# Squares of the first halves of w1 and w2: ScalarE sums instead of TensorE diagonals, in a fused attention and MLP kernel

## The chip, the cores and the metric

The kernel runs on one core of a Trainium2 chip. A core has five engines, each with an in-order queue of its own: TensorE (PE in the profile; its weight loads are listed apart, as PEld), VectorE (DVE), ScalarE (ACT), GpSimd (POOL) and SyncE (SP, which here issues nearly all DMAs). Matrix products write to PSUM, which has eight banks here called dense0 to dense7; everything else lives in SBUF. The engines wait for one another through semaphores. The metric is the device time of one execution in microseconds; the median of several runs counts.

## The reference

One call computes, for 2048 tokens of width 512,

```
xn  = layernorm(x)
A   = infini_attention(xn, wq, wk, wv, beta) @ wo      # 32 heads of 16, 4 segments of 512 tokens
B   = gelu(layernorm(xn) @ w1 + b1) @ w2 + b2          # w1: 512 x 1792, w2: 1792 x 512
out = x + A + B
```

In the attention each segment has a masked softmax of its own; a memory matrix per head, summed over the segments before, is read with phi(q) and mixed in with sigmoid(beta).

The kernel keeps full accuracy by splitting each float32 matrix into a high and a low float16 half (h and l) and by taking three products, hh, hl and lh. Before a weight is split it is scaled by a power of two, and that power comes from the sum of the squares of the weight's elements. These sums are what the change is about. They do not appear in the reference.

## The kernel before

**Stages.** In the head of the kernel the weights are loaded, their squares summed, the power of two worked out, and the pieces scaled and split. At the same time the first tokens are normalised (`ln`, `norm_*`), turned by TensorE (`ln_out`, line 564) and split into xnT. Then the work is: projections of q, k and v (`qk_proj`, `v_nat`, line 586 through `split3`), row maxima of the logits (`m_job`, line 744 on TensorE, 751 on VectorE), softmax exponentials (`s_job`, lines 786 and 793), the product with v (`pv`, line 820), the hidden layer (`d_job`, line 586 on w1), gelu (`gelu`, line 895), its split (`h_split`), the second layer (`e_jobs`, line 935) and the output projection (line 955). Attention is cut in 16 units (4 segments by 4 groups of 8 heads); the MLP in 16 units (8 blocks of 256 tokens by two halves of the 1792 hidden columns). "1a" and "2a" are the first halves of w1 and w2 (7 of 14 pieces of 128 x 512 each), "1b" and "2b" the second halves.

**The order.** Each job has a key, such as ("D", 0, 3). `streams()` makes one list of keys per kind of job, and the string ORDER says, one letter for each job, which list gives the next job. Jobs are emitted in that order, so every engine's queue is a cut through it: an engine runs its own parts in the order of the string, and waits where an input is not there yet. BANKS gives the PSUM bank of each job in the same way. There is no scheduler at run time; where a job stands in the string is decided offline.

**Warm-up jobs.** 24 jobs ("W", function `warm`, line 500) are products of the identity with itself, two of 256 columns each. Their result is never used. They too have places in ORDER.

**Squares.** `w_square(m, k)` sums the squares of one piece. For "qk", "1b", "2b", "o" and the bias b1 it is one ScalarE ACTIVATE with the function Square and an accumulator (line 353), followed by a READ_ACCUMULATOR. For the parts in TRACES it is `w_trace`: each 128 x 128 block is taken as bfloat16 (the upper halves of its float32 words) and multiplied by itself on TensorE (line 382), all blocks into one PSUM bank; the sum of squares of each column is then on the diagonal, and one VectorE operation with the identity (line 384) takes it off. Part 1a has two such jobs of 14 blocks each, after its DMAs, and the b1 square; part 2a two jobs of 16 and 12 blocks.

**Scales and splits.** `w_scale(m)` ("wf") adds the column sums over the partitions with a product with ones (line 414, and 416 for b1), and works out the scales on VectorE in a chain of small operations (lines 388 to 438). `w_split` ("ws") then makes h and l of each piece: a "V" piece by ScalarE (line 447) and VectorE (line 448), a "G" piece by GpSimd (450), ScalarE (452) and GpSimd (454). In 1a and 2a the pieces 0, 2, 4 and 6 are "G" and 1, 3 and 5 "V".

**The queues of the head, before.** With the names of the keys (T and Tp projections of q and k, second number 1 for k; V projections of v; Xt turned tokens; D hidden layer; M row maxima; N turned phi(k); Cb rows of ratios; wm squares; wf scales; ws splits; par2 small constants), ORDER gives:

```
PE : W.0..W.15 Xt.0.0.0 W.16 wf.qk W.17 Xt.0.0.1 wm.QK.0 wm.v.0 W.18..W.20 wm.v.1 wm.QK.1 wf.v W.21 Cb.0 wm.QK.2 W.22 W.23
     Tp.1 V.0.0 wm.QK.3 wm.QK.4 par2.0 wm.QK.5 V.0.1 Xt.0.1.0 Tp.0 wf.QK Xt.0.1.1 Cb.1 wm.1a.0 wm.1a.1 T.0.1 wf.1a T.0.0
     T.1.0 wm.2a.0 wm.2a.1 D.0.0 wf.2a D.0.1 .. D.0.6 M.0.0 M.0.1 M.0.2 N.0 T.1.1 ..
ACT: wm.qk.0 wm.qk.1 Xt.0.0.0 Xt.0.0.1 ws.qk.0 ws.qk.1 ws.v.0 ws.v.1 Cb.0 ws.v.2 ws.v.3 V.0.0 V.0.1 Xt.0.1.0 Xt.0.1.1 Cb.1
     ws.QK.1 ws.QK.0 wm.1a.2 (b1) T.0.1 T.0.0 ws.1a.0 ws.1a.1 T.1.0 ws.1a.2 ws.QK.3 ws.1a.3 .. ws.1a.6 ws.2a.3 G.0 ..
SP : x(2) wv(1) qk(2) QK.0(2) v.1(2) QK.1(2) x(2) QK.2(2) beta b1 1a(4) 2a(2) ..
```

The split of a weight can begin only after its wf, and D.0.f needs the split piece f of 1a. S.0.0, the first softmax job, and everything behind it come later, from 66 us on.

Of the kernel before, what the change touches and what calls it, by code (L numbers as in the profile page):

```python
# [9 lines left out]
F32 = mybir.dt.float32  # L10
# [49 lines left out]
def streams():  # L60
# [78 lines left out]
    "hxahhhlhk6hkkhwxbhhlchkhdhhe6hhhfh6auhfi8$hks7hhl$8$h7%%j%8%hbhgRtc88dmr8ieRfg8fmjn&v9&9!&y&#9(nCzA)((CD++*)X9"  # L139
    "+2*BB((D)o,!-*X(,(X3)*,X,9.XoXXYZ#0F1FFPy-,FZz.0Fp1F,R49F/oZF4-.!0R,1-.Z4F//F4XABXB#0Q/F4$4/=p14=4PUE44FF::4;="  # L140
    "=4G<4GFGX=FG2XG3FHF22:4;HI>:IHq?aIIFGb@:GXc>XGH>FGyFFGXXz?d:<fFeYXC;HHAEZXIQIDI0I><GGG>J1HXX:>KX4GBBLGZfP0MHCF"
    "FHqQNOIII1;IDGF44GGFiZ<0[34X>1GaZFFyHF@?zGF4H4@X0?FBFHIY@I1I3bI4c[4A4[FEJBK4XZ40X1X4ZX0[1L44GGGXXGFeF4Z4d0HffP"
    "1a4FZGF4H4]H014FYMFF44N]Z4yFzQOIIjII]0GF4CAF]G4XD4TFEXbGG1G4^B4PHHHZB0XIIII_GJ1GKGXHVyFZLG0Gz4i41C4AHFFIHTMNI^"
    "IZOIDG01G44XHXGF44GFGHXBFFYFIHIIIBFFRR4_FFFF44X44EGZJF0KLc1GX4MNOHR4iSZeGGGRdFHH0FIII1QIFZFGSGFFUPHyAGUG5HzGSX"
    "FWS2EI0H1BIIQ53IGGJVZKLC2DGTGGXX4MHPN0WX444VBHfHOfIIIQIFGF44GG14XFG3GY4HjH4HZ04FFF4yF1F5IaIIIZFz0F4CX41bX42DXX"
    "F4BEJZ4401X4Z0cTXXKe14ABU5344i4XYdGZGLF4XMGFF4H440UGF2G414ZHNPXFFIHIOIIQ0GGFX3XGG1HFXWFFZGH0f44fVF1ZHX4Y4y04E1"
    "IzIZIIJGG44KCA4LG0aGG4BHDjTMNH44H4W44OI1IIBIGGGXVXbPGHFGZyFFzHFHIIIcI0R1AJRZF01KZFFLRCFFFX0BRDeXFdfEfBX4X44GM1"
    "GGH4aU4NT4XFGGOS4FHFYFQHIIIIWXFZ5GFSP04G1G4X4FZbGGS4H2HFFH0FIQIIiI1yzZS0FJKVEAcCT4D4LXGMG4PX1BHGUGGNZX3X444HWV"
    "0HIIBIOIGF5G41444GFGXFGjF2yFHzHFHFIYQZeIII0JCK4U41ZUTX4DBX40FF3dF1Z4X041XLX4FZ0f45M1X4EWVA44Bf4N45GGG4X4FFGYHX"
    "4O4ZFGHF44H2440XPFFI1IIIFFGZy20F1ZGHF44XX04z13GG3ZHG4FHCXXTX0414UIEjIDQYIIBJGGK444GGHLGMBHX4Z4XXXINIHIOIFGF401"  # L150
# [8 lines left out]
    "01234567012345670123456713072134627341257034275036125470361254370125403725340725364072316420731460271024637102"  # L159
    "46530274163045127301245701367205136472013642713642076143201746317204617240672406532146532710465372104573201457"  # L160
    "32014562014205634205136420571360257143026714302514307251403751264037521640375231640723164073164072536140725361"
    "40275430612754130675421630542631054261054327654132764153276415032761450376145076145076152074153674316507431650"
    "71436257143263527014305127643207516320753620741625074136250741253607451320745130267451360245136042513674251367"
    "45213670452103647210364720364507326450732640532647032614750326174032641073256417023546170354617305617305614307"
    "61423076513427364517351062473510625417365241760524176024576102437610243716024375413602154376021576403157640135"
    "74061357406135671403275164032751643027543402751340257136402731640273674301274360136274103764214032765403276510"
    "327650413615304651302451243705124037254137254012375640213574021734502617350261735406"
# [17 lines left out]
def infini_mixer_kernel(ctx: ExitStack, tc: tile.TileContext, x, wq, wk, wv, wo, beta, w1, b1, w2, b2, out):  # L185
# [65 lines left out]
    AM = {"v": 8, "1a": 10, "1b": 12, "2a": 17, "2b": 19, "o": 23}  # L251
    am = cst.tile([P, 28], F32, name="am")
# [74 lines left out]
    def w_square(m, k):  # L327
        if m in TRACES and (m, k) != ("1a", 2):
            return w_trace(m, k)
# [3 lines left out]
        else:  # L333
            to = am[:, AM[m] + k:AM[m] + k + 1]
            a = m[0]
            if m == "1a" and k == 2:
                r, to = b1t, am[:, 16:17]
            elif m[1:] == "a":
                r = flat(a)[:, 1024 + 1792 * k:2816 + 1792 * k]
            elif m[1:] == "b":  # L340
                o = 1024 + 512 * FH
                r = flat(a)[:, o + 1536 * k:o + (1536, 2560)[k]] if k < 2 else stage[a][k - 2]
            elif k == 0:
                r = flat(a)[:, 1024:2048]
            else:
                r = stage[a][2 if m == "v" else k - 1]
# [6 lines left out]
        A.activation(junk.bitcast(BF)[:, :r.shape[1]], r, AF.Square, accum_out=to)  # L353
# [3 lines left out]
    def w_trace(m, k):  # L357
# [50 lines left out]
    def w_scale(m):  # L408
# [6 lines left out]
        if m == "1a":  # L415
            T.matmul(p[:, 1:2], ones, am[:, 16:17], start=True, stop=True)
# [642 lines left out]
```

## Time and profile before

| | |
|---|---|
| median of 3 runs | 690.71 us (690.51 to 691.18) |
| the profiled execution's own time | 689.64 us |
| span of the profile | 687.9 us |
| TensorE busy | 680.4 us (99%), 5883 products |
| VectorE / ScalarE / GpSimd busy | 502.6 / 472.7 / 348.9 us |
| granted TensorE clock | 0.998 over the span |
| HBM read / written | 37.77 / 17.05 MB |

The span is the time from the first to the last instruction in the trace; the device time holds some 1.7 us more. A product on TensorE is shown with the time from its start until its result is out, and the next one begins before that; so a group's time in a list (twelve products of 256 columns: 1.47 us) holds one such tail, and the cost of one more product in a row is read from two groups of different counts. A busy TensorE is thus not a TensorE without gaps; whether it waits is read from the list of waits and from the chain that ended last. For an instruction with an idle time before it, the list gives that time in brackets with what ended it.

### The profile page before, as it was taken

How to read it: one execution, taken by the hardware profiler on the slowest of the kernel's cores; microseconds unless marked ns; L12 is line 12 of the kernel's file. 1: busy time of each engine (PE TensorE's matmuls, PEld its weight loads, DVE VectorE, ACT ScalarE, POOL GpSimd, SP SyncE). 2: the span in 40 equal slices, each digit the busy share in tenths (PEclk: the TensorE clock that was granted, in tenths of full speed). 3: DMA queues.
4: the chain of work that ended last, by engine and by line, in shares of the span. 5: the costliest groups of instructions: out<-in, count | busy, mean ns of one | idle time of the engine just before them, and what ended most of it. 6: DMA issues, size and time to landing. Idle time of an engine off the chain costs nothing.

```text
span 687.9 us, 15912 instructions
## 1 busy us (share of the span) xinstructions
PE 680.4 (99%) x5883; PEld 393.8 (57%) x5883; DVE 502.6 (73%) x1615; ACT 472.7 (69%) x877; POOL 348.9 (51%) x574
## 2 busy tenths in 40 slices
PE   8999999999999999999999999999999999999997
PEld 6765664666554666665545555665654446475543
DVE  5899968897896668786595786977477765787522
ACT  4588998787856666678826747666956545857960
POOL 5595769664536354563652426435363325247562
PEclk9999999999999999999999999999999999999999
DMA  9788243222120441512222023330502122240001
GB/s 276 225 209 238 82 113 93 64 63 73 57 39 16 109 117 36 121 17 80 55 61 81 16 72 78 85 88 20 114 24 63 56 65 77 62 102 17 4 16 61
DMA packets 52890, 55.85 MB, mean 81 GB/s; under 512 B 4990, under 2 KB 41868, under 8 KB 52812
## 3 DMA queue, kind: packets, MB, share of 16 engines
q1 hardware_dynamic: 50508, 50.64, 26.9%
q0 software_dynamic: 2304, 4.20, 3.8%
q8 instruction: 46, 0.75, 0.5%
q14 instruction: 32, 0.26, 0.1%
HBM read 37.77 MB, written 17.05 MB: 80 GB/s over the span
## 4 chain that ended last, share of the span: by engine, by line
PE 96%; DVE 1%; DMA 1%; POOL 0%; ACT 0%; issue 0%; SPq 0%; POOLq 0%; DVEq 0%
PE dense L586 40%; PE dense L935 21%; PE dense L820 11%; PE dense L744 6%; PE dense L786 6%; PE dense L955 6%; PE dense L684 2%; PE dense L564 1%; DMA wqs<-in_A_wq_dram 1%; PE dense L700 1%; PE dense L651 1%; PE dense L382 1%; PE dense L721 1%; PE dense L757 0%; DVE xnT L568 0%
## 5 line engine op out<-in xcount | busy, mean ns | idle before, releaser
L751 DVE CUSTOM_DVE_ANT_0 dense<-dense,mask 128x384 f32<-128x384 f32 (+3 forms) x512 | 233.8, 528 | 28.5 <-PE dense L744 24.3
L793 ACT ACTIVATE pt<-dense,qkcs 128x512 f32<-128x512 f32 (+1 forms) x384 | 204.3, 628 | 45.1 <-PE dense L786 44.7
L935 PE MATMUL dense<-w2s,hT 128*128 128x512 f16 x672 | 166.7, 380 | 0.0
L586 PE MATMUL dense<-xnT,w1s 128*128 128x256 f16 x1344 | 160.0, 273 | 0.0
L807 POOL TENSOR_SCALAR_AFFINE_SELECT pt<-pt 128x256 f32<-128x256 f32 x256 | 100.3, 424 | 109.3 <-ACT pt L793 108.8
L586 PEld LDWEIGHTS <-w1s 128*128 128x128 f16 x1344 | 129.3, 98 | 29.4 <-issue 5.9
L909 POOL TENSOR_TENSOR hT<-hh,hT 128x512 f16<-128x512 f32 x64 | 67.2, 1050 | 101.4 <-ACT hT L907 89.6
L935 PEld LDWEIGHTS <-hT 128*128 128x128 f16 x672 | 60.8, 98 | 68.0 <-issue 14.0
L820 PE MATMUL dense<-pt,vt 128*32 128x512 f32 (+3 forms) x1024 | 77.2, 436 | 0.0
L751 DVE DVE_READ_ACCUMULATOR2_ANT mc<- 128x1 f32 x512 | 73.9, 144 | 0.0
L888 DVE SCALAR_TENSOR_TENSOR hT<-dense,sc,cb 128x512 f32<-128x512 f32 x64 | 43.6, 681 | 33.8 <-PE dense L586 33.5
L820 PEld LDWEIGHTS dense<-pt,vt 128*32 128x32 f32 x1024 | 31.4, 109 | 40.9 <-issue 32.4
L786 PE MATMUL dense<-qst,kst 50*128 50x384 f16 (+3 forms) x512 | 52.0, 298 | 0.0
L744 PE MATMUL dense<-kst,qst 48*128 48x384 f16 (+3 forms) x512 | 51.9, 298 | 0.0
L905 POOL TENSOR_SCALAR hh<-hT,sc 128x512 f32<-128x512 f32 x64 | 42.3, 661 | 17.5 <-ACT hT L895 11.4
L851 POOL TENSOR_TENSOR nN<-nN,oT 128x512 f32<-128x512 f32 x16 | 20.3, 1272 | 52.6 <-DVE oT L663 52.6
L907 ACT ACTIVATE hT<-hh 128x512 f16<-128x512 f32 x64 | 37.5, 585 | 13.7 <-POOL hh L905 13.7
L895 ACT ACTIVATE hT<-hT,b1t 128x256 f32<-128x256 f32 x112 | 46.5, 498 | 0.2
L955 PE MATMUL dense<-wos,oT 128*128 128x512 f16 (+2 forms) x204 | 44.0, 367 | 0.9 <-DVE acc L957 0.7
L586 PE MATMUL dense<-xnT,wks 128*128 128x512 f16 (+1 forms) x252 | 44.4, 329 | 0.0
L586 PE MATMUL dense<-xnT,wqs 128*128 128x512 f16 (+1 forms) x252 | 44.2, 328 | 0.0
L586 PE MATMUL dense<-wvs,xnT 128*128 128x512 f16 x192 | 43.6, 379 | 0.0
(229 smaller groups left out, 836.9 us busy)
## 6 DMA issues: line engine op xcount, KB each, us to landing
kst<-kd SPq DMA_DIRECT2D x32, 192.0 KB
qst<-qd SPq DMA_DIRECT2D x32, 192.0 KB
qd<-hl SPq DMA_DIRECT2D x36, 128.0 KB
kd<-hl SPq DMA_DIRECT2D x33, 128.0 KB
acc<-in_A_x_dram SPq DMA_DIRECT2D x16, 256.0 KB
acc<-in_B_b_dram POOLq DMA_DIRECT2D x16, 256.0 KB, 4.5
out_dram<-acc SPq DMA_DIRECT2D x15, 256.0 KB
xt<-in_A_x_dram SPq DMA_DIRECT2D x14, 256.0 KB
```

The source lines that it names most:

```text
L586: T.matmul(p, ws(k, a), xs(k, b), start=i == 0, stop=i == 3 * KT - 1)
L744: T.matmul(p[:, o:o + n], stk[i, 0][r, t, P * qb:P * qb + P], stk[i, 1][r, t, :n], start=True, stop=True)
L751: V.tensor_tensor_reduce(p[:, o:o + n], p[:, o:o + n], mask[:, 512 - n:], 1.0, -3e38, OP.add, OP.max, mc[i][:, 4 * b + t, qb:qb + 1])
L786: T.matmul(p[:, o:o + n], stk[i, 1][r, t, P * kb:P * kb + P], stk[i, 0][r, t, P * kb:], start=True, stop=True)
L793: A.activation(pt[i, 4 * b + t][:, OFF[kb]:OFF[kb] + n], p[:, c:c + n], AF.Exp, scale=qkcs[:, 1, i % NG:i % NG + 1])
L807: G.affine_select(v, v, pattern=[[0, 2], [1, P]], compare_op=OP.is_ge, fill=0.0, base=0, channel_multiplier=-1)
L820: T.matmul(p[32 * c:32 * c + 32, P * kb:], vt[s, kb][:, 4 * g + c, 16 * odd:16 * odd + 32], pt[i, 2 * c + odd][:, OFF[kb]:OFF[kb] + LEN[kb ...
L888: V.scalar_tensor_tensor(hz[:, f0:f + 1, :], p[:, :256 * n].rearrange("p (f c) -> p f c", f=n), col(CG + fh), cbt[hf].unsqueeze(1).to_broa ...
L895: A.activation(hz[:, f, :], hz[:, f, :], AF.Gelu_apprx_tanh, bias=b1t[:, fo:fo + 1])
L909: G.tensor_tensor(hT[:, z, 1, :], hht[j, c], hT[:, z, 0, :], op=OP.subtract)
L935: T.matmul(p, t[:, u, P * a:P * a + P], w2s[:, fo, v, :], start=fi == 0 and n == 0, stop=fi == FH - 1 and n == 2)
L955: T.matmul(p[:, c], o[:, u, P * b:P * b + P], wos[:, g, v, c], start=i == 0, stop=i == 3 * NG - 1)
```

## The change

TRACES keeps only QK and v. The squares of 1a are now four ScalarE sums, one for each of the four DMAs of 1a (128 rows of w1 each; on the chip seven runs of 128 elements per partition, 896 in all), and the b1 square is the fifth job of the part. Those of 2a are two ScalarE sums, one for each DMA (2048 and 1536 elements per partition). `am`, the tile of partial sums, has three more columns. In `w_scale` the product with ones now takes four columns for 1a and two for 2a where it took one, and a VectorE reduction adds these (`n > 1`). The 56 products of blocks and the two operations that took the diagonal off go.

ORDER and BANKS are new for the first 391 jobs (393 in the new string); the remaining 1330 jobs stand in the same order. The number of warm-up jobs is the same.

```
-TRACES = ("QK", "v", "1a", "2a")
+TRACES = ("QK", "v")
-SQUARES = {"qk": 2, "QK": 6, "v": 2, "1a": 3, "2a": 2, "1b": 4, "2b": 4, "o": 3}
+SQUARES = {"qk": 2, "QK": 6, "v": 2, "1a": 5, "2a": 2, "1b": 4, "2b": 4, "o": 3}
-    AM = {"v": 8, "1a": 10, "1b": 12, "2a": 17, "2b": 19, "o": 23}
-    am = cst.tile([P, 28], F32, name="am")
+    AM = {"v": 8, "1a": 26, "1b": 12, "2a": 17, "2b": 19, "o": 23}
+    am = cst.tile([P, 31], F32, name="am")
...
-        if m in TRACES and (m, k) != ("1a", 2):
+        if m in TRACES:
             return w_trace(m, k)
...
-            if m == "1a" and k == 2:
-                r, to = b1t, am[:, 16:17]
-            elif m[1:] == "a":
-                r = flat(a)[:, 1024 + 1792 * k:2816 + 1792 * k]
+            if m == "1a":
+                r, to = (flat(a)[:, 1024:1024 + 512 * FH].rearrange("p (f r c) -> p f r c", f=FH, r=KT)[:, :, k], to) if k < 4 \
+                    else (b1t, am[:, 16:17])
+            elif m == "2a":
+                r = flat(a)[:, 1024 + 2048 * k:(3072, 1024 + 512 * FH)[k]]
...
-        A.activation(junk.bitcast(BF)[:, :r.shape[1]], r, AF.Square, accum_out=to)
+        junk = junk.bitcast(BF)[:, :r.shape[1] * (P if len(r.shape) == 3 else 1)]
+        if len(r.shape) == 3:
+            junk = junk.rearrange("p (f c) -> p f c", c=P)
+        A.activation(junk, r, AF.Square, accum_out=to)
...
-        n = 4 if h else 3 if m == "o" else 1
+        n = 4 if h or m == "1a" else 3 if m == "o" else 2 if m == "2a" else 1
...
-            T.matmul(p[:, 1:2], ones, am[:, 16:17], start=True, stop=True)
+            T.matmul(p[:, 4:5], ones, am[:, 16:17], start=True, stop=True)
```

The new ORDER gives these queues in the head:

```
PE : W.0..W.9 Xt.0.0.0 W.10 W.11 Xt.0.0.1 wm.QK.0 W.12 wf.qk W.13 wm.v.0 wm.QK.1 wm.v.1 wf.v wm.QK.2
     Tp.1 wm.QK.3 wm.QK.4 Cb.0 V.0.0 wm.QK.5 V.0.1 wf.QK Xt.0.1.0 Xt.0.1.1 par2.0 W.14..W.16 Tp.0 T.0.1 T.0.0 W.17 W.18
     wf.1a W.19..W.23 T.1.0 Cb.1 N.0 D.0.0 D.0.1 wf.2a D.0.2 .. D.0.5 M.0.0 D.0.6 M.0.1 M.0.2 M.0.3 T.1.1 ..
ACT: wm.qk.0 Xt.0.0.0 wm.qk.1 Xt.0.0.1 ws.qk.0 ws.qk.1 ws.v.0 .. ws.v.3 Cb.0 V.0.0 wm.1a.0 wm.1a.1 V.0.1 Xt.0.1.0 Xt.0.1.1
     ws.QK.1 wm.1a.2 ws.QK.0 wm.1a.3 T.0.1 wm.1a.4 (b1) T.0.0 wm.2a.0 ws.1a.0 ws.1a.1 wm.2a.1 ws.1a.2 ws.1a.3 ws.QK.2 T.1.0
     Cb.1 ws.1a.4 N.0 ws.1a.5 ws.QK.3 ws.2a.1 ws.2a.0 ws.1a.6 G.0 ..
DVE: .. Xt.0.0.0 Xt.0.0.1 wf.qk par2.1 wm.v.1 ws.qk.0 wf.v ws.qk.1 ws.v.0 ws.v.1 wm.QK.4 ws.v.2 ws.v.3 ..
SP : x(2) wv(1) qk(2) QK.0(2) v.1(2) QK.1(2) QK.2(2) x(2) 1a(2) beta b1 1a(2) 2a(2) ..
```

On GpSimd the first norm root (X.0.0.2) now comes ahead of the memset of the ones in vt (const.2); before it came behind it.

66 lines of the change are left out of this document (28 added, 38 removed).

## The prediction

> **What bounds the kernel now.** I read the page first, then the list of who waited for whom on TensorE, then the chain that ended last for the first 45 us, which is where the order changes. From the page, the chain by engine, and the complete list of TensorE's waits:
>
> ```profile
> span 687.9 us, 15912 instructions
> PE 96%; DVE 1%; DMA 1%; POOL 0%; ACT 0%; issue 0%; SPq 0%; POOLq 0%; DVEq 0%
> ...
> PE dense L500 <- POOL ident masks.py:199: 1.4, 1, 1.4
> PE dense L564 <- DVE xt L535: 1.0, 1, 1.0
> PE dense L955 <- DVE acc L957: 0.7, 1, 0.7
> PE dense L414 <- DVE dense L384: 0.3, 1, 0.3
> ```
>
> Columns of the waits: total us, times, longest. TensorE waits four times, 3.4 us in all; three of the four lie in the first 13 us. Behind them it works without a wait up to the last stage. So what counts is the sum of TensorE's work, warm-ups included. The chain of the first 45 us (start, length, what; count of instructions):
>
> ```profile
> 2.70 5.93 DMA wqs<-in_A_wq_dram
> ...
> 11.88 0.66 DVE wks L448
> ...
> 13.48 0.22 PE dense L527 x2
> ...
> 24.38 1.60 PE dense L382 x28
> ...
> 31.56 1.60 PE dense L382 x28
> 33.16 1.31 PE dense L586 x12
> 34.47 0.12 PE dense L414 x2
> 34.59 7.88 PE dense L586 x72
> 42.47 0.76 PE dense L744 x8
> 43.23 0.58 PE dense L651 x4
> ```
>
> Until about 9 us the path is the load of q's weights; from 14 us it is TensorE, and the two blocks of 28 products that the change removes (L382 on w1s and w2s) stand on it with 1.60 us each. The order of time of TensorE shows what warm-ups fill and what they cost (start, length, what, count):
>
> ```profile
> 1.43 6.18 PE L500 MATMUL dense<-ident 128*128 128x256 bf16 x32 [1.43 <-POOL ident masks.py:199]
> 8.62 0.63 PE L564 MATMUL dense<-ident,xt 128*128 128x128 f32 x4 [1.01 <-DVE xt L535]
> 9.09 0.38 PE L500 MATMUL dense<-ident 128*128 128x256 bf16 x2
> ...
> 11.03 0.82 PE L500 MATMUL dense<-ident 128*128 128x256 bf16 x6
> ...
> 14.20 1.47 PE L586 MATMUL dense<-xnT,wks 128*128 128x256 f16 x12
> ```
>
> Two products take 0.38 us and six 0.82, so one more costs (0.82 - 0.38) / 4 = 0.11 us and one warm-up job 0.22 us. Tp.1, the first projection, starts at 14.20 us behind all 24 warm-up jobs.
>
> Finally the other engines by stretch, and ScalarE's queue around the change:
>
> ```profile
> 10.00:20.00 10.00, 9.68 (x91) 7.20 (x90) 9.00 (x30) 5.35 (x9) 2.16 (x7) 1.00 1.16 310
> 20.00:30.00 10.00, 10.00 (x95) 8.07 (x94) 7.97 (x33) 5.45 (x12) 5.85 (x10) 1.00 0.75 246
> 30.00:40.00 10.00, 10.00 (x101) 8.48 (x99) 8.80 (x19) 7.17 (x13) 8.54 (x8) 1.00 0.75 179
> 40.00:50.00 10.00, 9.98 (x71) 5.58 (x70) 9.04 (x34) 9.53 (x18) 9.09 (x11) 1.00 0.83 217
> 50.00:60.00 10.00, 10.00 (x98) 5.58 (x97) 9.96 (x40) 8.49 (x18) 7.78 (x9) 1.00 0.96 262
> ...
> 18.30 0.60 ACT L711 ACTIVATE vt<-dense 128x512 f32<-128x512 f32 x1 [1.70 <-PE dense L586]
> 21.84 0.60 ACT L711 ACTIVATE vt<-dense 128x512 f32<-128x512 f32 x1 [2.94 <-PE dense L586]
> ...
> 24.20 0.60 ACT L567 ACTIVATE xnT<-dense 128x512 f16<-128x512 f32 x1 [1.27 <-PE dense L564]
> ...
> 35.09 0.63 ACT L452 ACTIVATE w1s<-w1s 128x512 f16<-128x512 f32 x1 [1.15 <-POOL w1s L450]
> ...
> 40.22 1.28 ACT L895 ACT_TABLE_LOAD   x1
> ...
> 51.08 1.47 ACT L353 ACTIVATE w1s<-w1s 128x1536 bf16<-128x1536 f32 x1
> 52.45 0.19 ACT L353 ACTIVATION_READ_ACCUMULATOR w1s<-w1s 128x1 f32 x1
> ...
> 55.65 1.04 ACT L353 ACTIVATE w1s<-w1s 128x1024 bf16<-128x1024 f32 x1
> ```
>
> Columns of the stretches: length, then busy us of PE, PEld, DVE, ACT, POOL, granted clock, DMA share, GB/s. ScalarE is idle for 4.65, 4.55 and 2.83 us in the three stretches from 10 to 40 us, 12.0 us together; from 40 us it is nearly as full as VectorE and TensorE. Three limits lie close together there.
>
> **The change, part by part.**
>
> *Products removed:* 2 x 1.60 = 3.20 us of TensorE, all of it on the chain. The two reductions of `w_scale` stay off it: the sums over four and two columns are added on VectorE, 0.2 us each at most (a small operation, below), against two removed diagonal operations; the product with ones takes four columns for one at the same count. I take 0 for both. Their cover is VectorE's idle 1.2 us of 30 to 40; without it they would cost 0.4.
>
> ```profile
> 26.20 0.29 DVE L384 SCALAR_TENSOR_TENSOR dense<-dense,ident 128x128 f32<-128x128 f32 x1
> 26.41 0.14 DVE L384 DVE_READ_ACCUMULATOR dense<-dense,ident 128x1 f32 x1
> ...
> 19.21 0.16 DVE L973 TENSOR_REDUCE eo<-half 128x2 f32<-128x8 f32 x1
> ```
>
> *Warm-ups moved:* the count is the same, but W.14 to W.23 now stand behind Tp.1: 10 x 0.22 = +2.2 us on a TensorE that does not wait there. This is the term that takes most of the gain back. It costs nothing only where TensorE would have waited anyhow; it is worth all of 2.2 where it would not.
>
> *Tp.1 earlier:* fewer jobs stand ahead of it. What it waits for is the low half of k's first piece on VectorE, done at 11.88 + 0.66 = 12.54 us before. In the new order VectorE has the small constants and v's diagonal ahead of that operation (about 0.6 and 0.35 us), so about 13.5 us, and Tp.1 at 13.6: -0.6 us. On GpSimd the norm root no longer sits behind the memset of vt (1.07 us), so the first turned tokens come about 1.3 us sooner, but the sum of q's squares waits for its load in any case. Bounds: -1.1 (13.1, when v's diagonal hides) and +0.5 (below).
>
> ```profile
> 3.68 1.07 POOL L229 MEMSET vt<- 128x256 f32 x4
> ...
> 6.85 0.24 POOL L483 TENSOR_SCALAR nw<-ag 128x2 f32<-128x2 f32 x1
> ```
>
> *Cb.0 behind Tp.1:* two turned rows, 0.22 us (L527 above): +0.2. N.0 and M.0.0 come ahead of D.6 and would have to be done anyway: 0.
>
> *Loads:* SP's queue has q's and k's last pieces ahead of the second pair of x, and beta and b1 between the DMAs of 1a. The bytes ahead of w2's last piece are the same and the queue streams without a gap; the page of 12 to 30 us in 40 slices of 0.45:
>
> ```profile
> GB/s 330 347 346 340 339 300 296 293 309 287 288 299 298 264 295 300 281 273 280 310 238 211 287 289 339 355 373 396 355 387 405 373 287 159 146 46 0 0 50 132
> ```
>
> It ends near 28 us. One DMA of 1a (448 KB, at about 290 GB/s) takes some 1.6 us; the products read the last one at 24.2, so the four are there by about 19.4, 21.0, 22.6 and 24.2 at the latest, and 2a by 28. The turned second tokens need x two pieces later (512 KB, some 1.7 us); VectorE reaches that x at 17.3 us before and not sooner now, so I take 0, and +0.3 for the one place where I see TensorE wait: between V.0.1 and the turned second tokens, whose norm follows v's splits on VectorE. Bounds 0 and 1.
>
> *ScalarE's new work:* from the rows with 1536 and 1024 elements one element costs (1.47 - 1.04) / 512 = 0.84 ns, and from 51.08 to the instruction behind the read at 52.55 is 1.47 us, so the read is nearly hidden. A sum of 896 costs 0.95 us, of 2048 1.9, of 1536 1.47: 4 x 0.95 + 1.9 + 1.47 = 7.2 us, into 12.0 us of idle time. The pieces of w1 land one after another, and the first two sums lie in the wait of 2.94 us ahead of the second V. Behind them queue, in order, the turned tokens, the splits of q and k, T.0.1 and T.0.0; the two sums of 2a stand right among the splits of 1a. I put ScalarE's queue together from 23.3 us (the split ws.QK.1, behind the second turned tokens) to the split ws.1a.6: eleven splits at 0.52 to 0.6 (6.3 us), four sums and b1's (5.6), T.0.1, T.0.0, T.1.0, Cb.1 and N.0 (2.9), and the rest of the starts, 15.7 us in all, so 39.0 us if it waits for nothing. GpSimd needs some 1.2 us more for the low half of piece 6: 40.2. TensorE wants it at D.0.6. That job began at 34.59 + 7.88 - 1.31 = 41.16 before; the sum below, with N.0 (0.58) and half of the M products (0.4) now ahead of it, puts it at about 41.0. So ScalarE's cover is 0.8 us: hidden, with little left.
>
> *Sum:* -3.2 + 2.2 - 0.6 + 0.2 + 0.3 = -1.1 us. The profiled execution took 689.64 us, 1.07 below the median of the runs shown, so it would be 688.5 there, and **689.6 us** against the median of 690.71. The rest, from 43 us on, has the same work; I see no wait in the old order there, so the new one can win nothing by order alone, except from VectorE's side, a rival below.
>
> *The clock, by the rows and by a rule.* The first 32 warm-up products take 6.18 us: (6.18 - 0.38) / 30 = 0.19 us for each, where later ones take 0.11. So TensorE starts slow. Now only 20 such products run, from 1.43 to about 5.3 us, and then TensorE pauses until about 7.3 (8.62 less the 1.3); if it is slow still, the jobs up to Tp.1 (8 turned blocks, 4 warm-ups, 28 products of blocks: some 4 us at the fast rate) take up to 3 us more, of which about 1 would be on the way to Tp.1; from these rows I carry 0, with +1.05 as the upper end. The Trainium skill ("TensorE: Matmul & The Clock Gate", Part 1) says that the array runs at half rate until it has been busy through one free-running window of about 3.4 us. By that rule the shorter burst may miss its window, and the fast rate may come only between 10 and 14 us: an estimate from that page would be a sum of -0.1 instead of -1.1. The row agrees that the start is slow; no row shows what a pause does to it.
>
> **The rivals.**
>
> *A, the forecast:* TensorE stays the bound, -1.1, from -1.8 to -0.4.
>
> *B, VectorE was the real limit from 43 us on, and it comes forward.* For it: 9.96 of 10 us busy from 50 to 60. The first row maximum now needs D.0.5 and not D.0.6 and N.0: TensorE reaches M.0.0 1.31 us sooner on top of 1.1, minus 0.58 for N.0, and the last product of D.0.6 is then VectorE's to do later (0.5). Against it: TensorE shows no wait there, and cannot lose work by it. It gives about -1.9, 688.8 us.
>
> *C, the saving is given back in the head:* the slow clock, or ten warm-ups plus a wait. It gives about -0.1, 690.6 us: the order does what it says, nothing is won.
>
> *D, ScalarE's queue becomes the bound.* Its place is the stretch from T.0.1 to D.0.6; its price is one for one what ScalarE waits there beyond 0.8 us. For it: before, it was idle for 2.83 us of 30 to 40 alone, and 1.27 us in one wait ahead of that, each time for an engine that is no faster now, and the sums of 2a delay the splits behind them by 3.4 us. Against it: with more work queued, a wait turns into work. At 3.3 us of waits it gives 3.3 - 0.8 - 1.1 = +1.4 and decides for slower; at 3.7, less than those two together, +1.8, 692.5 us.
>
> **How the numbers follow.** A change of 0.2%, 1.4 us, is about what measuring this kernel can tell from none. A has 0.36, and a third of it (0.11) lies beyond -1.4; B 0.20; C 0.24; D 0.20. Faster: 0.11 + 0.20 = 0.31. Same: 0.25 + 0.24 = 0.49. Slower: D, 0.20. The likeliest case by itself reaches from 688.9 to 690.3. For the range I take the lower bounds of Tp.1 and of the wait, and B's gain, together about -2.9 (687.8), and above D's 692.5: 687.8 to 692.5 leaves out the far ends of B and D, some 2 in 10.
>
> **What would show it.** The two groups of 28 products are gone, and TensorE is busy 3 us less or so. Tp.1 starts near 13.6 and not at 14.2; D.0.6 begins near 41. There is no idle time of TensorE between Tp.1 and D.0.6 beyond the 0.3. ScalarE has four sums of 896 near 0.95 us, is busy some 7 us more before 40 us, and loads the gelu table near 39 to 40. Rival C would show in the clock: warm-up and turned products at 0.19 us and more up to 11 us and beyond. D would show idle time of TensorE ahead of D jobs, released by GpSimd's or ScalarE's split of w1s. The prediction is wrong if TensorE waits by more than 1 us anywhere between 15 and 130 us, where before it never does, or if the ten warm-ups lie in time that would have been idle.

## The result, and the profile after

The changed kernel took 695.92 us (median of 6 runs, 695.55 to 700.42) against 690.63 for the kernel before on the same chip: ratio 1.007, 95% interval 1.0043 to 1.0097. Run again with more rounds it took 696.5 against 691.24 (ratio 1.0083, 1.0056 to 1.011). It is slower by some 5 us; 689.6 was forecast, with 692.5 as the upper end.

The first profiled execution of the changed kernel was its slowest (700.42). So the reading below goes by the profile of `e1_changed_again` (696.02 us), where not said otherwise. Most code lines of the changed kernel are six below those of before (586 is 580 there, 744 is 738; ScalarE's squares are 357 for 353); those of e10 and e11 are four above. Its page, with the span and the chain by engine:

```profile
span 694.3 us, 15813 instructions
...
PE 87%; DVE 5%; DMA 3%; ACT 1%; SPq 1%; issue 1%; POOL 1%; POOLq 0%; DVEq 0%; ACTq 0%
```

Its list of who waited for whom on TensorE (total us, times, longest), without what lies in the first 14 us and two entries of 0.3 and 0.2 us at its end:

```profile
PE dense L715 <- ACT vt L705: 1.6, 1, 1.6
...
PE dense L580 <- DVE phk L632: 1.2, 1, 1.2
...
PE dense L645 <- DVE phk L632: 0.7, 1, 0.7
PE dense L949 <- DVE acc L951: 0.7, 1, 0.7
PE dense L738 <- DVE mc L745: 0.7, 1, 0.7
PE dense L780 <- DMA qst<-md: 0.6, 1, 0.6
```

The chain was 96% TensorE before; now 87%, with more of VectorE (5% for 1%) and DMA (3% for 1%) in it. Before, TensorE had one wait behind 13 us, the 0.7 at the end. Now there are two above 1 us, and they are of other kinds: V.0.3 (L580) waits for VectorE, K.0 (L715) for ScalarE. Busy times in stretches of 10 us (length, then PE, PEld, DVE, ACT, POOL, granted clock, DMA share, GB/s):

```profile
10.00:20.00 10.00, 8.97 (x80) 6.20 (x81) 9.00 (x32) 6.39 (x12) 1.48 (x5) 1.00 1.12 303
20.00:30.00 10.00, 10.00 (x83) 8.09 (x82) 6.99 (x31) 9.71 (x21) 6.09 (x10) 1.00 0.89 288
30.00:40.00 10.00, 9.26 (x78) 7.47 (x77) 7.87 (x16) 9.62 (x17) 7.06 (x8) 1.00 0.66 181
40.00:50.00 10.00, 9.78 (x70) 5.34 (x69) 10.00 (x30) 8.19 (x15) 8.19 (x9) 1.00 0.60 162
50.00:60.00 10.00, 7.20 (x79) 3.88 (x74) 9.97 (x29) 6.29 (x12) 6.04 (x8) 1.00 0.97 251
```

TensorE is idle for 2.8 us of 50 to 60, where before it had 10.00; VectorE is full from 40 on. ScalarE has the forecast work in 20 to 40 and is *less* busy behind it than before: it waits there too.

Where the time goes is read from TensorE's start on named jobs. The table has the time of before and, for each profiled execution, how much later (+) or earlier (-) it starts. At D.0.6 the new order has N.0 and M.0.0 (about 1 us) already done; from M.1.0 on the jobs done are the same, and from about 128 us the order of TensorE is.

| us | Tp.1 | D.0.6 | M.1.0 | at 128 | last product |
|---|---|---|---|---|---|
| before | 14.20 | 41.00 | 64.10 | 128.1 | 684.02 |
| changed (e1) | -0.34 | +0.70 | +3.09 | +5.11 | +6.66 |
| e6, warm-ups first | -0.81 | -0.44 | +0.77 | +1.94 | +2.91 |
| e12, and early load | -0.23 | +0.15 | -0.34 | +0.79 | +2.24 |
| e15, and old order from M.1.0 | +0.06 | -0.14 | -0.78 | -0.58 | +1.08 |
| e17, changed, old order from M.1.0 | -1.02 | +0.01 | +2.38 | +3.22 | +3.32 |
| e10, old order, no squares | +0.35 | -1.17 | +1.28 | +1.72 | +2.16 |
| e11, and early load | +1.22 | -0.30 | +0.07 | +0.10 | +0.36 |
| e13, before with early load | +0.47 | +0.47 | +0.46 | +0.45 | +0.53 |

Each row is one execution. Those of e10 (691.81) and e17 (693.0) are the shortest of their kernels, 2.1 and 2.2 us below the median, so what their other executions lost beyond the row is not seen.

So the head of e1 came out near the forecast: D.0.6 at 41.70 for about 41, which is 0.3 us won, jobs done ahead included, where 1.1 was forecast. The loss has three places: 43 to 64 us, 64 to 128 us, and about 1.5 us behind that.

### The profile page after: what moved, and what is told of

It is laid out like the page before. It is cut to its first block, busy times and chain, and to the rows that moved or that the text cites. A ratio compares the mean times of both kernels' runs of the same rounds, so it can differ in the third digit from the quotient of the medians.

```text
span 698.7 us, 15813 instructions
## 1 busy us (share of the span) xinstructions
PE 682.5 (98%) x5827; PEld 392.4 (56%) x5827; DVE 508.0 (73%) x1613; ACT 478.8 (69%) x889; POOL 347.1 (50%) x574
## 4 chain that ended last, share of the span: by engine, by line
PE 88%; DVE 4%; ACT 2%; DMA 2%; POOL 2%; issue 1%; POOLq 0%; SPq 0%; ACTq 0%; DVEq 0%
PE dense L580 35%; PE dense L929 19%; PE dense L814 10%; PE dense L949 6%; PE dense L780 6%; PE dense L738 5%; PE dense L678 2%; PE dense L558 1%; DVE dense L745 1%; PE dense L694 1%; PE dense L645 1%; DMA xt<-in_A_x_dram 1%; DVE w2s L442 1%; POOL kst L239 1%; PE dense L715 0%
## 5 line engine op out<-in xcount | busy, mean ns | idle before, releaser
L745 DVE CUSTOM_DVE_ANT_0 dense<-dense,mask 128x384 f32<-128x384 f32 (+3 forms) x512 | 233.8, 527 | 31.7 <-PE dense L738 25.5
L580 PE MATMUL dense<-xnT,w1s 128*128 128x256 f16 x1344 | 160.4, 273 | 0.0
L580 PEld LDWEIGHTS <-w1s 128*128 128x128 f16 x1344 | 129.3, 98 | 29.9 <-issue 6.1
L929 PEld LDWEIGHTS <-hT 128*128 128x128 f16 x672 | 61.2, 98 | 68.8 <-issue 15.5
L580 PE MATMUL dense<-wvs,xnT 128*128 128x512 f16 x192 | 43.7, 379 | 1.2 <-DVE phk L632 1.2
L580 PE MATMUL dense<-xnT,wks 128*128 128x512 f16 (+1 forms) x252 | 44.4, 329 | 0.2 <-DVE mc L745 0.2
L580 PE MATMUL dense<-xnT,wqs 128*128 128x512 f16 (+1 forms) x252 | 44.4, 329 | 0.0
```

The source lines that it names most:

```text
L580: T.matmul(p, ws(k, a), xs(k, b), start=i == 0, stop=i == 3 * KT - 1)
L745: V.tensor_tensor_reduce(p[:, o:o + n], p[:, o:o + n], mask[:, 512 - n:], 1.0, -3e38, OP.add, OP.max, mc[i][:, 4 * b + t, qb:qb + 1])
L929: T.matmul(p, t[:, u, P * a:P * a + P], w2s[:, fo, v, :], start=fi == 0 and n == 0, stop=fi == FH - 1 and n == 2)
```

## The experiments

**The changed kernel again, and its two parts alone.** `e1_changed_again` is unchanged.

> The changed kernel as it is, for a second profile, since the profiled execution took 700.42 us and the median of its runs was 695.92. Theory P (port): three VectorE instructions with two SBUF operands or in a fast form (L626 at 49.2, the low half of w2's piece 3 at 52.7, C2 of wf.2b at 74.8 us) are held while GpSimd works back to back, and TensorE waits behind each; it expects 695.5 to 696.5 us and at least two of these three stretched again, to over twice their usual length. Theory Q (load): ScalarE's 7.2 us of new squares make it the bound behind the head; it expects ScalarE without idle time between 45 and 75 us and TensorE's waits released by ScalarE.

Measured: 696.5 (695.26 to 701.72), as above. Two of the three operations that theory P names are stretched again (1.40 and 2.52 us, below); the third took 1.10. ScalarE has idle time, 3.47 us in one wait (below), where theory Q expected none.

`e2_new_order_products` keeps the new ORDER, and the products on TensorE:

```
-TRACES = ("QK", "v")
+TRACES = ("QK", "v", "1a", "2a")
+    # all 28 blocks at the last of a part's squares jobs; the b1 square stays on ScalarE
```

> The new order, but the squares of 1a and 2a as products on TensorE again (all 28 blocks where the last square stood) with the two diagonal operations; ScalarE has its old load. Q expects the waits behind 43 us to vanish: 690.6 + 3.2 - 1.1 = 692.7 us. P expects that the VectorE instructions of the order stay beside GpSimd's runs and that the waits stay: 698 to 700 us, 3 more than the changed kernel.

`e3_old_order_squares` is the other half: the old ORDER, the squares on ScalarE at the landings.

```
 old ORDER, new TRACES and SQUARES
-.. Cb.1 wm.1a.0 wm.1a.1 (b1) T.0.1 wf.1a T.0.0 T.1.0 wm.2a.0 wm.2a.1 D.0.0 wf.2a D.0.1
+.. wm.1a.0 wm.1a.1 V.0.1 .. wm.1a.2 Tp.0 .. wm.1a.3 (b1) T.0.1 T.0.0 wf.1a wm.2a.0 T.1.0 wm.2a.1 D.0.0 D.0.1 wf.2a
```

> The old order and its banks with all warm-ups ahead of Tp.1, and the squares of 1a and 2a on ScalarE: the jobs of the squares, wf.1a and wf.2a are moved to where the pieces have landed, T.0.0 and D.0.1 ahead of them, nothing else. Q expects 7.2 us more on ScalarE to cost as in the changed kernel: 692 us or more. P expects the old neighbourhood of VectorE and GpSimd behind 43 us to stay clear: 690.6 - 3.2 + some 1.7 of waits at D.0.0 and D.0.2 = 689.1, between 687.5 and 690.5.

Measured: 694.37 (ratio 1.0055, 1.0034 to 1.0076) and 696.44 (1.0075, 1.0052 to 1.0097). Each half alone is slower than before, and the new order is 2.1 us *faster* with the products on TensorE than with the squares on ScalarE. e2 lies between what the two theories expected, and 1.7 us above the 692.7 that the forecast's own terms give, with no wait of TensorE above 0.7 us behind 14 us. e3 lies 7 us above theory P's 689.1. For the squares in the old order, TensorE's waits say why:

```profile
PE dense L580 <- POOL w1s L448: 2.7, 2, 2.2
PE dense L408 <- ACT w1s L357: 1.7, 1, 1.7
...
PE dense L408 <- ACT w2s L357: 0.8, 1, 0.8
```

The first and the third lie in the head: the splits of w1 come too late for D jobs, and wf.2a waits for the square of w2. The second lies at 66 us, in wf.1b, and returns below.

**The squares left out.** Is TensorE's work in the head worth anything? Two kernels do no squares of the first halves at all. Their partial sums are constants, so the scales do not come from the data:

```
+    G.memset(am[:, 10:11], 0.173)   # e10; the like for 1a and 2a in e9
...
+        if m == "2a" or m == "1a" and k < 2:
+            return
```

> The new order with the squares of 1a and 2a left out altogether: the columns of partial sums are filled with a constant of about their size by three small memsets at the start, so ScalarE has 7.2 us less to do and TensorE no products. Q expects the waits behind 43 us gone and 690 us or less. P, as far as it holds the order itself at fault, expects 694 to 696; a P in which the squares only shift VectorE's operations beside GpSimd's runs expects other waits than in the changed kernel, in sum smaller, 691 to 694.

> The old order with the products of 1a and 2a left out and the partial sums filled with constants, nothing in their place: the most that this change could win. If TensorE's work is what counts in the head, as my sum has it, 690.6 - 3.2 = 687.4 us. If another engine's chain (wf.1a and the splits on ScalarE, VectorE and GpSimd) stands right behind TensorE there, less: 688.5 to 690.6, with waits of TensorE at D jobs.

Measured: 693.26 in the new order (1.0031, 1.0013 to 1.005) and 693.92 in the old one (1.0039, 1.0017 to 1.0061). So in the new order the squares on ScalarE cost some 3 us against none at all (e1 against e9, 696.5 and 693.26), as much as was to be saved on TensorE. It shows behind the head: from D.0.6 to M.1.0, with the same jobs in the same order, the profile of e9 takes 23.1 us, that of e2 23.5 and that of e1 25.5.

e10 came out above all that was expected of it. It is the run that overturns the forecast's premise: 3.2 us of TensorE's work are taken out of the old order, nothing is put in, and the kernel gets 3.0 us *slower*. The table shows how: from Tp.1 to D.0.6 it is 1.5 us faster; by M.1.0 it is late. ScalarE, TensorE and SP's queue of that run (start, length; waits: total, times, longest):

```profile
60.21 0.63 ACT L357 ACTIVATE w1s<-rc 128x512 bf16<-128x512 f32 x1 [4.18 <-DMA rc<-in_B_w_dram]
```

```profile
62.01 0.38 PE L418 MATMUL dense<-am,ones 128*128 128x4 f32 x2 [1.79 <-ACT w1s L357]
```

```profile
SPq L312 <- DMA kd<-rc: 3.4, 1, 3.4
```

The same in the kernel before:

```profile
57.14 0.63 ACT L353 ACTIVATE w1s<-rc 128x512 bf16<-128x512 f32 x1 [0.35 <-DMA rc<-in_B_w_dram]
```

```profile
SPq L310 <- DMA kd<-rc: 1.7, 1, 1.7
```

TensorE waits in wf.1b, the scale of w1's second half, for the square of a piece that is loaded into the tile rc. That tile also carries a projection on its way to DRAM. So SP's queue may issue the load only when the store kd<-rc is done, and ahead of the load stand 1.28 MB of w2. Before, the last of these squares was done at 59.3 and wf.1b began at 60.8:

```profile
60.84 0.28 PE L414 MATMUL dense<-am,ones 128*128 128x4 f32 x2
```

In e10 SP waited longer for the store, and the piece came 3 us later: 0.9 us of it because the load was issued later (53.03 for 52.15), the rest between issue and landing. And TensorE came sooner. In both kernels the DMA engines are full meanwhile; the stretches 54 to 60 of e10 (columns as above):

```profile
54.00:56.00 2.00, 2.00 (x18) 1.00 (x17) 2.00 (x9) 2.00 (x4) 2.00 (x3) 1.00 1.03 334
56.00:58.00 2.00, 2.00 (x21) 1.79 (x19) 2.00 (x13) 0.03 (x1) 2.00 (x3) 1.00 1.04 237
58.00:60.00 2.00, 2.00 (x42) 0.98 (x40) 1.97 (x8) 0.00 (x0) 0.14 (x1) 1.00 1.04 205
```

A DMA share of 1.03 to 1.04, and ScalarE with nothing to do.

**The waits of the changed kernel.** Its longest ones follow VectorE operations that took far longer than their like. VectorE and GpSimd of `e1_changed_again`:

```profile
49.29 1.40 DVE L626 TENSOR_SCALAR phk<-phk,qksc 128x512 f32<-128x512 f32 x1
...
52.82 2.52 DVE L442 SCALAR_TENSOR_TENSOR w2s<-w2s,sc 128x512 f16<-128x512 f32 x1
```

```profile
49.24 1.16 POOL L903 TENSOR_TENSOR hT<-hh,hT 128x512 f16<-128x512 f32 x1 [1.71 <-ACT hT L901]
...
52.01 1.66 POOL L444 TENSOR_SCALAR w2s<-w2s,sc 128x512 f32<-128x512 f32 x2
53.35 1.43 POOL L448 TENSOR_TENSOR w2s<-w2s 128x512 f16<-128x512 f32 x1
```

and TensorE behind them:

```profile
51.47 2.75 PE L580 MATMUL dense<-wvs,xnT 128*128 128x512 f16 x12 [1.21 <-DVE phk L632]
...
58.10 0.27 PE L715 MATMUL dense<-vt,pkn 128*32 128x32 f32 x8 [1.59 <-ACT vt L705]
```

The first VectorE operation begins 0.05 us behind a GpSimd instruction and ends 0.3 us behind its end; the second begins beside two and ends 0.56 us behind the end of the third. V.0.3 waits for the first by way of VectorE's next operation (L632). K.0 waits for the second by way of ScalarE, which stands still for it and then has a split and a square of w1's second half to do ahead of the copy that K.0 needs:

```profile
55.37 0.72 ACT L441 ACTIVATE w2s<-w2s,sc 128x512 f16<-128x512 f32 x1 [3.47 <-DVE w2s L442]
```

The same jobs in the same order, some 2 us sooner, in `e6_warmups_first` (below):

```profile
47.58 0.48 DVE L626 TENSOR_SCALAR phk<-phk,qksc 128x512 f32<-128x512 f32 x1
...
50.19 0.98 DVE L442 SCALAR_TENSOR_TENSOR w2s<-w2s,sc 128x512 f16<-128x512 f32 x1
```

There V.0.3 and K.0 do not wait. The pair of 1.40 and 2.5 us between 48 and 59 us is in all profiles of kernels that have the squares on ScalarE and warm-ups behind Tp.1 (e1, e4, e14, e17 and the first profile; e5 has the 1.40 alone) and in none of e2, e6, e9, e12, e15 and e16. The Trainium skill ("SBUF — State Buffer", Who interferes with whom) has VectorE and GpSimd share a port pair, which VectorE takes in its two-port modes and of which it uses the reading side for a second SBUF input; whoever issues first holds it for a whole instruction. These rows agree, and show more: the hold here spans several GpSimd instructions in a row. That a shared port is what holds these operations is read from the overlap in time; no run parted it from other causes. And a held operation by itself need not cost: before has one of 1.58 us for a usual 0.7 (L448, at 26.41 us), and no wait of TensorE behind it.

Two runs took such waits away. In the first profile one such operation, a scale of 128 x 1, took 2.84 us where its like take 0.2 (and 1.10 us in e1, the same kernel):

```profile
74.80 2.84 DVE L432 SCALAR_TENSOR_TENSOR sc<-sc 128x1 f32<-128x1 f32 x1
```

`e4_c2_one_operand` gives it one SBUF tensor operand:

```
-            V.scalar_tensor_tensor(col(C2 + h), col(f), float(2 ** -26), col(B1F + h), op0=OP.mult, op1=OP.mult)
+            V.tensor_scalar(col(C2 + h), col(f), float(2 ** -26), col(B1F + h), op0=OP.mult, op1=OP.mult)
```

> The changed kernel, and only C2 (one column, f * 2^-26 * b1f) computed with the second factor as a scalar operand instead of as a second tensor from SBUF; same result, same order. P expects this instruction at 0.2 to 0.3 us in place of up to 2.84, TensorE's wait of 2.4 us at 76 to 79 us gone, and 693.5 to 694.5 us. Q expects no change: 695.9.

`e5_three_apart` is e4, and in addition V.0.3 and K.0 exchange their banks, and two splits of w2 on VectorE and GpSimd move behind the load of w1's last pieces:

```
-.. M.0.4 ws.2a.3 H.0.2.0 A.0.1 H.0.2.1 wl.1b.2 M.0.5 ws.2a.4 M.0.6 Tr.1.1 ws.2a.5 ..
+.. M.0.4 H.0.2.0 A.0.1 H.0.2.1 wl.1b.2 M.0.5 M.0.6 Tr.1.1 ws.2a.3 ws.2a.4 ws.2a.5 ..
-K.0 and V.0.3: banks 4 and 6
+K.0 and V.0.3: banks 6 and 4
```

> The changed kernel with the three places of TensorE's waits behind 43 us taken apart and nothing else: V.0.3 and K.0 exchange their PSUM banks (V.0.3 no longer waits for the k tile of Tw.1.1), the split of w2's piece 3 stands three jobs later, next to that of piece 5, and C2 has a scalar operand. Theory P (VectorE instructions held beside GpSimd's runs, TensorE waits behind them): the low half of piece 3 back from 2.5 to under 1.2 us, the waits of 1.2, 1.6 and 0.7 us gone, 696.0 - 3.5 = 692.5 us in executions in which the clock stays fast. Theory Q (ScalarE's load): the waits come back at neighbouring jobs, 695 to 696.5.

Measured: 696.27 (1.0067, 1.0043 to 1.0091) and 696.38 (1.0076, 1.0051 to 1.0101): nothing won. In the profile of e4 the operation took 0.21 us, and the 2.51 stayed; in that of e5 the 2.5 was gone as well, but other waits had come in its place, at the neighbours:

```profile
PE dense L580 <- DVE mc L745: 3.0, 2, 2.8
PE dense L715 <- ACT vt L705: 1.1, 1, 1.1
PE dense L738 <- ACT pt L787: 0.9, 1, 0.9
```

So taking these waits away by themselves won nothing, and in e5 they moved. That they moved because VectorE is full there fits the busy times, but no run gave VectorE less to do.

**The warm-ups.** `e6_warmups_first` puts all 24 ahead of Tp.1 and changes nothing else:

```
-.. W.9 Xt.0.0.0 W.10 W.11 .. W.13 .. Tp.1 .. W.14 W.15 W.16 Tp.0 .. W.17 W.18 wf.1a W.19 .. W.23 T.1.0 ..
+.. W.9 .. W.15 Xt.0.0.0 W.16 W.17 .. W.18 wf.qk W.19 .. W.20 W.21 .. W.22 W.23 wf.v .. Tp.1 ..
```

> The changed kernel with all 24 warm-up jobs ahead of Tp.1 again: 16 ahead of the first turned tokens, the others in TensorE's waits between there and wf.v; nothing else moves. My sum priced the ten warm-ups behind Tp.1 at 2.2 us on a TensorE that does not wait: 693.8 us. If they stood in waits anyway: no change in the undisturbed executions, 695.5 to 696.5. Either way, if the slow clock of the head makes the executions at 698 us and above, these go, and the granted clock shows no half-rate stretch before 20 us.

Measured: 692.87 (1.0031, 1.0017 to 1.0045), 3.6 us less than the changed kernel. The table splits the 3.8 us between the two profiles: 0.5 by Tp.1, 0.7 on to D.0.6, 1.2 on to M.1.0 (the two waits above are gone; a wait of 1.59 us in wf.1b has come), and 1.4 from there to the end. The granted clock is 1.00 in the heads of both, and their turned blocks take 0.60 us, so none of this is the clock. In other executions of the changed kernel it is. That kernel has 20 warm-up products at its start and then waits for the first tokens; before and in e6 there are 32. The first profile of the changed kernel, TensorE and the stretch behind it (last columns: granted clock, DMA share, GB/s):

```profile
7.66 0.79 PE L558 MATMUL dense<-ident,xt 128*128 128x128 f32 x4 [2.36 <-DVE xt L529]
```

```profile
8.00:12.00 4.00, 4.00 (x30) 0.58 1.14 322
```

and the same stretch of e1:

```profile
8.00:12.00 4.00, 2.91 (x37) 1.00 1.15 324
```

Behind a wait of 2.36 us the clock is 0.58. In e14 it was 2.22 us and 0.54, in e4 1.97 and 0.60, while in e1, with 1.80 us, it stayed at 1.00, and so it did in e17 (1.95) and in before (1.01). In e9, with 1.90 us, four turned blocks took 1.06 us for a usual 0.60 as late as 9.5 us, though the clock reads 1.00 there. So the length of the wait alone does not decide it. This is rival C's mechanism: it struck in four of the eight profiles with 20 products at the start (the others: e1, e2, e5, e17), and Tp.1 came at 15.0 to 15.5 us in three of these four. The forecast carried 0 for it.

**The load of w1's last pieces.** Four kernels take away what this load waits for: it goes to two tiles that are free then, and right behind the other loads of w1's second half.

```
-                stage["1"] = [sb.tile([P, 512], F32, name=t)
-                               for t in ("rc", "ame")]
+                stage["1"] = [sb.tile([P, 2, 512], F16, name="oT", bufs=4).rearrange("p a c -> p (a c)").bitcast(F32)
+                              for j in range(2)]
-.. wl.1b.1 .. wl.2b.0 .. wl.1b.2 ..
+.. wl.1b.1 wl.1b.2 .. wl.2b.0 ..
```

(The expectation of e11 speaks of wf.1a where wf.1b is meant.)

> The order of before without products or squares of the first halves (their partial sums are constants, so the output is not the reference's, as in the run e10_old_order_no_squares), and in addition the loads of the last two pieces of w1 go into two tiles of the tag oT instead of the tags rc and ame, and are issued right behind the other loads of w1's second half. In e10_old_order_no_squares these two loads waited 3.4 us on SP's queue for the store kd<-rc out of the same tile, stood behind 1.28 MB of w2, and ScalarE idled 4.18 us and TensorE 1.8 us (at wf.1a's second part, L418) for them. Theory L (what TensorE saves in the head is lost at w1's second half, because its last two pieces land too late): the square of rc starts ahead of 57 us (60.2 before this edit), the wait of 1.8 us is gone, M.1.0 starts at 63.3 (65.4 less 2.1), time 691.8, that is within 0.3% of before and 2.1 below 693.92. Theory N (every engine is about as full, a wait that is removed turns up at a neighbour): M.1.0 at 64.5 or later, time 693.2 or more.

> e6_warmups_first (692.87: the changed kernel with all 24 warm-ups ahead of Tp.1) with the same move of the loads of w1's last two pieces. There TensorE waited 1.6 us at L408 for the squares of these pieces and ScalarE 1.4 and 0.75 us for their landing. Theory L: the wait is gone, 691.3 (692.87 less 1.6). Theory N: 692.3 to 693.4.

> The kernel before with the same move of the loads and nothing else. Its TensorE has no wait between 42 and 68 us, so theory L expects nothing to be won or lost: 690.9, within 0.7. Theory N in its strong form (the order of before is a point at which everything is aligned, and any shift costs): 692.5 to 695.

> The changed kernel with the same move of the loads and nothing else. In the profile of e1_changed_again ScalarE did not idle for these loads (it reached the square of rc 1.0 us after its last packet) and TensorE waited 0.5 us at L408. Theory L alone would have the loss of the changed kernel between 43 and 67 us (3.3 us) come from these loads: 693.2. Theory N, and the theory that ScalarE's own order is late there (its squares of w1's second half begin at 56.0 against 51.1 before): 695.5 to 696.5.

| | without | with the early load | ratio to before |
|---|---|---|---|
| e11, old order, no squares | 693.92 (e10) | 690.51 | 0.9994 (0.9986 to 1.0003) |
| e12, changed, warm-ups first | 692.87 (e6) | 691.38 | 1.0027 (1.0003 to 1.0051) |
| e13, before | 690.82 | 691.25 | 1.0016 (0.9995 to 1.0036) |
| e14, changed | 696.5 (e1) | 696.52 | 1.0081 (1.0062 to 1.01) |

ScalarE's square of the piece in e11, and in e12:

```profile
56.92 0.63 ACT L357 ACTIVATE w1s<-oT 128x512 bf16<-128x512 f32 x1
```

```profile
58.26 0.62 ACT L357 ACTIVATE w1s<-oT 128x512 bf16<-128x512 f32 x1
```

No idle time in brackets any more, and no wait in wf.1b in either list. The load theory holds in all four: -3.4 and -1.5 us where the wait was, nothing in before, which had none, and nothing in the changed kernel, where the waits at V.0.3 and K.0 cover this one. (The two profiles of e10 and e11 differ by 1.8 us, as much as the wait; the rest of the 3.4 has no profile.) That e13 stays within 0.5 us, and in its profile carries a shift of 0.47 us from Tp.1 to 128 us unchanged, also speaks against the view that any shift of the old order costs. And e11 against e13, 0.7 us, is the most that leaving the squares out is worth in the old order once its wait is gone, not 3.2; the intervals overlap, and the two profiled executions differ by 0.2. Of the 3.2, 1.7 is lost on the way to D.0.6 already, for from Tp.1 to there e10 and e11 are 1.5 us faster than before.

**The order behind M.1.0.** `e15_old_order_from_m1` is e12 as far as M.1.0 and the old ORDER and BANKS from there; `e17_changed_old_order_from_m1` is the same with the changed kernel for e12; `e16_head_waits_moved` is e15 with two more moves:

```
 e15, e17: .. e.0.1.2 [new ORDER to here] Z.4 Rr.0 M.1.0 M.1.1 ws.1b.0 ws.1b.1 e.0.1.3 .. [as before]
 e16:
-.. wm.1a.3 .. T.0.1 Tv.0.1 wm.1a.4 (b1) T.0.0 ..       -.. N.0 D.0.0 D.0.1 wf.2a ..
+.. wm.1a.3 wm.1a.4 (b1) .. T.0.1 Tv.0.1 T.0.0 ..       +.. D.0.0 D.0.1 N.0 wf.2a ..
```

> e12_warmups_early_load as far as M.1.0 (TensorE's start on it: 63.8 us there, 64.1 in the kernel before), and from M.1.0 on the order and banks of the kernel before instead of the new ones (they differ as far as about 128 us; what is done by M.1.0 is the same in both but for Z.4 and Rr.0, which come first now). In e12 TensorE was 0.34 us ahead of before at M.1.0, 0.8 behind at 128 us and 2.2 behind at the end, of it 1.2 at S.4.0 (203 us), where a store of row maxima landed late. Theory O (the new order between 64 and 128 us itself costs about 1.1 us, and 2.0 in the changed kernel): 690.3 (691.38 less 1.1), at 128 us ahead of before by 0 to 0.5 us. Theory P (any order costs the same here, the loss follows from the state that is handed on at M.1.0): 691.0 to 692.

> e15_old_order_from_m1 with two more moves in the head: the square of b1 right behind those of w1's first half (TensorE waited 0.56 us for it at L410), and N.0 behind D.0.1 (TensorE waited 0.79 us for phk ahead of N.0, and 0.47 us ahead of D.0.0's second part for a split of w1). If the saving in the head now reaches the end: 0.5 to 1.2 us below e15, that is 689.1 to 689.8, and the first version below the kernel before. If something else holds D.0.6 or M.1.0 by then (loads, VectorE): within 0.3 us of e15.

> The changed kernel as far as M.1.0 and the order and banks of before from there on; no other edit. In e1_changed_again TensorE was 3.1 us behind before at M.1.0, 5.1 at 128 us and 6.7 at the end. Theory O: the 2.0 us between M.1.0 and 128 us go, 694.1 (696.0 less 2.0). Theory P: 695.5 to 696.5.

Measured: e15 690.13 (0.9981, 0.9966 to 0.9996), e16 690.75 (0.9997, 0.9982 to 1.0012), e17 695.22 (1.0054, 1.0035 to 1.0072). So the new order behind M.1.0 costs about 1.3 us by itself, in both: 691.38 to 690.13 and 696.5 to 695.22. In the profiles the stretch from M.1.0 to 128 us shows 0.9 (e12 and e15) and 1.2 (e1 and e17). For e17 that is less than the 2.0 of theory O and more than theory P allows, and its interval overlaps that of e1. With all three repairs the change is a gain of 0.6 us; its interval (0.9966 to 0.9996) ends just short of 1.

e16 is a miss, and an instructive one. Its profiled execution is its longest (692.23). The two waits that it was to remove were gone there, and two others had come at D.0.0; TensorE of e16, its clock (column in front of the DMA share), and TensorE of e15:

```profile
30.91 0.39 PE L580 MATMUL dense<-xnT,w1s 128*128 128x256 f16 x2 [0.93 <-ACT w1s L446]
32.15 4.24 PE L580 MATMUL dense<-xnT,w1s 128*128 128x256 f16 x22 [0.85 <-POOL w1s L448]
```

```profile
30.00:32.00 2.00, 0.39 (x2) 1.00 0.53 165
32.00:34.00 2.00, 1.85 (x10) 0.60 0.87 254
34.00:36.00 2.00, 2.00 (x12) 0.54 0.86 216
```

```profile
32.43 2.78 PE L580 MATMUL dense<-xnT,w1s 128*128 128x256 f16 x24
```

TensorE idled for 1.6 us of 30 to 32, the clock fell, and 22 products took 4.24 us where 24 take 2.78: some 1.7 us lost behind two waits of 0.93 and 0.85. D.0.6 came at 42.47 and not at 40.86.

## Why the prediction was wrong

By its own steps:

- *Products removed, -3.2:* the two groups are gone (5827 products for 5883), though TensorE's busy time fell by only 1.2 us (679.2 for 680.4), where the prediction looked for 3. But the step rested on the sentence "So what counts is the sum of TensorE's work", and that is where it failed. e11 against e13 puts the removal at 0.7 us at most, e10 at +3.0 as the loads stood. TensorE had no wait between 14 and 682 us before, but the others had no room either. The stretches of before (columns as above):

```profile
43.00:48.00 5.00, 4.98 (x34) 2.41 (x31) 5.00 (x19) 4.97 (x10) 4.60 (x6) 1.00 0.90 233
48.00:53.00 5.00, 5.00 (x27) 2.18 (x26) 5.00 (x21) 4.59 (x8) 2.97 (x3) 1.00 0.51 156
53.00:58.00 5.00, 5.00 (x38) 2.87 (x36) 5.00 (x24) 4.28 (x10) 4.75 (x6) 1.00 1.11 337
```

VectorE has 5.00 of 5.00 us in each, ScalarE little less, the DMA engines 1.11 in the last, and wf.1b's last square had 1.5 us to spare. An engine that never waits was read as the only limit; it was one of several that met at the same time.
- *"The rest, from 43 us on, has the same work; I see no wait in the old order there, so the new one can win nothing by order alone":* it could lose. This is the step with the largest part of the error: +2.4 us between D.0.6 and M.1.0 in the table, 3.4 with the jobs that were done ahead (the two waits of 1.2 and 1.6 are most of it), and about 1.3 behind M.1.0 (e15, e17). These places overlap with the causes: e6 alone takes 1.2 of the 2.4 away.
- *Warm-ups moved, +2.2:* the term was mis-sized; e6 puts it at 3.6. What goes beyond 2.2 is, by the profiles, the shift by which VectorE's operations fall beside GpSimd's and, in some executions, the clock; the two were not separated. Conversely warm-ups behind Tp.1 may be worth something where waits come: e16 shows what the clock can do where nothing fills them, but no run put some there.
- *Tp.1 near 13.6, D.0.6 near 41:* 13.86 and 41.70. The wait of 0.3 forecast between them was one of 0.7, and not at the turned tokens but ahead of N.0.
- *ScalarE's new work:* right in every size, and hidden as far as D.0.6, but put at nothing for what comes behind; there it cost some 3 us in the new order (e1 against e9), and nothing that still shows with the three repairs (e15). Sums of 896 took 0.94 and 0.95 us, 2048 1.90, 1536 1.47; the gelu table's load began at 39.31. The rows of 896 and 2048:

```profile
19.18 0.94 ACT L357 ACTIVATE w1s<-w1s 128x896 bf16<-128x896 f32 x1
...
27.90 1.90 ACT L357 ACTIVATE w2s<-w2s 128x2048 bf16<-128x2048 f32 x1
...
39.31 1.28 ACT L889 ACT_TABLE_LOAD   x1
```

- *Rival D* (ScalarE's queue) had the sign and the wrong place: TensorE waits ahead of no D job for a split of w1 in e1. *Rival B* (VectorE is the limit from 43 us on) had the engine, by the busy times, and the wrong sign: where VectorE was full, the new order lost. *Rival C's* clock is in four of eight profiles. The prediction named its own refutation, a wait of more than 1 us between 15 and 130 us; there are two. The lower end of the range, put at 2.9 us below before, adds up to 2.7 from its own terms; nothing hangs on it.

What stays open: the 1.5 us that the changed kernel loses behind 128 us. About 1 us of it, in e1, e6, e12, e15 and others, comes at S.4.0, where a store of row maxima is late. SP's queue in before, and in e12:

```profile
SPq L767 <- DMA md<-mhl: 1.1, 1, 1.1
```

```profile
SPq L761 <- DMA md<-mhl: 3.1, 1, 3.1
```

The store md<-mhl takes 2.7 to 3.2 us there (and in e3, e5, e9, e14 and e16), and 1.1 in before, e2, e4, e10, e11, e13 and e17; the profiles do not say why. Why the old order is cheaper from M.1.0 to 128 us was not traced to single waits either. Single executions up to 698 us in e12 and e13 have no profile; the three above 697 have a granted clock of 0.993 to 0.995 over their span, where those below 692 have 0.998 to 1.000, so the clock was low somewhere in them.

## What to carry to other kernels

A list of waits with nothing in it says that the engine is a limit, not that it is the only one. Before pricing a saving on it, look how long each of its inputs had been ready (the idle time of the engines that feed it, the landing of the loads), and cap the gain there. And where an order is replaced, price the part with the same work too: here it lost more than the head could win. Take away the cover of a wait and the wait together: here the early load won nothing until the warm-ups had moved.

## What the runs showed of the hardware

- A VectorE operation that begins beside GpSimd's may be held through several instructions: 2.52 us for a usual 0.7, over three of them, and 2.84 us for a 128 x 1 operation of 0.2. (Read from the overlap in time.)
- The granted clock fell to 0.54 to 0.60 behind waits of TensorE of 1.97 to 2.36 us early in the kernel, and behind 0.93 and 0.85 us close together; waits of 1.80 and 1.95 us left it at 1.00. The Trainium skill ("TensorE: Matmul & The Clock Gate", Why this matters for your kernels) advises no gaps above some 3 us between bursts; by these runs that is not short enough.
